# Windowed attention and a gated two-layer network on one core: output weights loaded in one piece ahead of the second batch, and a new table of order biases

## The chip, the cores and the metric

The kernel runs on one core of a Trainium2 chip, as one program. The metric is the device time in microseconds (us), the median of the runs shown. All data start and end in the chip's DRAM; loads, casts, transposes and stores are inside the time.

## The reference

For 8 batches, 8 heads, 576 positions and a head size of 64, the scores are `q @ k.T / 8`. Heads 0 to 3 ("plain") keep the 32 positions up to and including the row's own; heads 4 to 7 ("dilated") keep every fourth one of the last 128. A softmax over what is kept and a product with `v` give x, seen as 4608 tokens of 512 features (8 heads by 64).

Then comes the network, with `w_in` 512 x 2048, `beta` of 2048 and `w_out` 2048 x 512:

```python
h = x @ w_in
g = h * (1.0 / (1.0 + np.exp(-beta * h)))
return (g @ w_out).astype(np.float32)
```

All inputs and the output are float32; the kernel computes in bfloat16 with float32 sums.

## The kernel before, in words

**Two streams of work.** The network takes the tokens in 9 tiles of 512. For tile t, `slot_h` makes 16 blocks of 128 hidden features ("Ht", four matmuls of 128x512 each, L919); ScalarE takes a tanh (L928) and VectorE the gate (L933). `block` makes four output blocks ("Ot.0" to "Ot.3", 16 matmuls each in four parts, L954), evacuated at L969 or L971 and stored at L974. The attention of batch b must be done before the tiles that hold its 576 tokens: H1 needs batches 0 and 1, H2 batches 1 and 2, H3 batches 2 and 3, H4 batches 3 and 4, and so on.

**Attention of one batch.** Queries and keys must have their feature dimension on the partitions. For batches 0 to 2 (`b < DIRECT`) POOL's queue loads rows into `st` (`direct_qk`, L418), and TensorE turns them in four groups of 36 small matmuls (L502 dilated, L512 plain; 64 rows each), evacuated at L259. For batches 3 to 7 POOL's queue casts q and k into a DRAM scratch `s` (`cast`), and SP's queue brings them back by a transposing DMA (`crossbar`, L490). Then come scores (L715 dilated, L684 the last 64 positions of the dilated heads, L743 and L779 plain), exponentials on ScalarE (L651), masks (L655), products with the values (L805, L820, L836) and the normalization on VectorE (L670, L671). In batches 0 and 1 TensorE turns the result back into `xT` (L858, L873, L888, put at L259). From batch 2 on `back_dma` writes x to DRAM scratch (L539, L547, L552) and reads it back transposed, in two halves (L566), on SP's queue.

**What sets the order.** Nothing is reordered at run time: each engine and each DMA queue runs its instructions in program order and waits on semaphores. The program order is made at build time by the class `Plan`. Every operation states its engines with an assumed duration, its dependences and a due value `vt`. `Plan.run` keeps a clock for each engine and takes, among the operations that could start next, the one with the smallest `vt` within a small window of the earliest start. `NUDGE` adds a bias in nanoseconds to the start of single operations, named by their number in the order of creation. It only decides who goes first, and on engines that can both do an operation also which one does it. `late` adds to the landing that the plan assumes for some loads (values, rows, transposed loads) from the fifth batch on (`b > DIRECT`). `SWITCH` is the time that the plan charges TensorE when it passes between matmuls of 64 rows and others, as told by `halves`. Where the plan sees TensorE idle it puts in a filler matmul (L1067, 128x256, of zeros). So all these values change the order of instructions and the number of fillers, and nothing else.

**Loads.** POOL's queue holds, in order: batch 0's rows, batch 0's values, `w_in` (three pieces), then two pieces of `w_out` (`w_out_ld`, half of it each) among batch 1's loads. The place of the two pieces is set by their `vt` of -7.235 and -7.19; batch 1's loads have -7.25 to -7.19. The loads of batches 3 to 7 wait for one small copy on POOL (`t_pace`, L1033): batch 3's for the gate of the first H1 block, later ones for the previous batch's transposed loads and for the rows of `xT` two batches back.

Of the kernel before, what the change touches and what calls it, by code (L numbers as in the profile page):

```python
# [23 lines left out]


class Op:
    def __init__(self, engs, fn, deps, vt, acquire, group, dma, lat, halves=0, sbuf=False):
        self.halves, self.sbuf = halves, sbuf
        self.engs, self.fn, self.vt, self.acquire = engs, fn, vt, acquire
        self.deps = [d for d in deps if d is not None]  # L30
        self.dma, self.lat, self.group = dma, lat, group
        self.end = self.ready = None
        self.bias = 0.0
        self.late = 0
        self.waits = 0
        self.next = []
        for g in group if isinstance(group, list) else [] if group is None else [group]:
            g.users.append(self)


class Plan:
# [2 lines left out]


    CAPS = {"h": 4, "p": 4, "o": 3, "z": 4, "a": 8, "s": 5, "w": 6}
    SWITCH = 105
    NUDGE = {22: -150, 26: -150, 34: -150, 48: 400, 50: 400, 58: 400, 70: -150, 72: 2500, 84: 900,
        85: -2500, 86: -2500, 88: 2500, 89: 2500, 95: 60, 96: -60, 102: 60, 105: 150, 116: 2500,
        117: 150, 130: 400, 149: -400, 155: -60, 159: 900, 161: -60, 176: -150, 181: -400, 185: 60,  # L50
        187: -60, 191: 150, 196: 2500, 208: 60, 221: 2500, 227: -150, 228: -2500, 242: 150,
        251: 900, 252: 2500, 262: 400, 273: -2500, 291: -2500, 301: 400, 302: 150, 305: 900,
        316: -150, 323: 900, 358: 2500, 359: -60, 363: -60, 370: 150, 380: -60, 381: 2500,
        385: 150, 387: 2500, 388: -900, 417: -900, 422: -150, 423: -900, 429: -400, 442: 400,
        497: -60, 516: -2500, 524: 900, 526: 150, 536: 400, 540: 900, 541: -400, 542: 900,
        545: -900, 547: -2500, 556: -400, 559: -400, 579: -2500, 585: 900, 588: 900, 598: -400,
        659: -400, 660: 900, 664: 150, 665: 2500, 673: -400, 674: 2500, 675: 150, 680: -400,
        682: -400, 701: 60, 702: -900, 704: -150, 753: -400, 798: -400, 804: 150, 805: 900,
        806: 150, 807: 900, 808: 400, 818: 2500, 929: -60, 1058: 60, 1078: -150, 1084: 150,
        1105: 150, 1267: 2500}  # L60
    LAT = {"PE": 210, "ACT": 45, "DVE": 45, "POOL": 60, "SP": 0}
    NEAR = {"PE": 40, "ACT": 60, "DVE": 60, "POOL": 60, "SP": 0}

    def __init__(self, banks):
        self.ops, self.banks = [], banks

    def op(self, engs, fn, deps=(), vt=0.0, acquire=None, group=None, dma=0, lat=None, halves=0, sbuf=False, late=0):
        acquire = acquire if acquire is None or isinstance(acquire, list) else [acquire]
        o = Op(engs, fn, deps, vt, acquire, group or acquire, dma, lat, halves, sbuf)
        o.late = late  # L70
        o.bias = self.NUDGE.get(len(self.ops), 0)
        self.ops.append(o)
        return o

    def run(self, filler=None, filler_until=0.0):
# [11 lines left out]
        n_left = len(self.ops)  # L87
        n_held = {k: 0 for k in self.CAPS}
        ends = []
        halves = 0  # L90
        issued = 0.0
        port = {"DVE": 0.0, "POOL": 0.0}

# [19 lines left out]
        while n_left:  # L113
# [29 lines left out]
            if filler is not None and s <= filler_until and free["PE"] + (300 if free["PE"] < COLD else 170) < s:  # L143
                now = free["PE"]
                open_banks = {x.bank for x in held.values()}
                spare = [b for b, t in bank_free.items() if b not in open_banks and t <= now]
                if spare:
                    filler(max(spare, key=lambda b: -bank_free[b]))
                free["PE"] = now + (225 if now < COLD else 115)
                halves = 0  # L150
                continue
            for g in o.acquire or ():
                open_banks = {x.bank for x in held.values()}
# [5 lines left out]
            if e == "PE" and o.halves != halves:  # L159
                halves = o.halves  # L160
# [40 lines left out]
def kernel(  # L201
# [11 lines left out]
    P = 128  # L213
# [22 lines left out]
    DIRECT = 3  # L236
# [333 lines left out]
    def attention(b, ld, names, vts):  # L570
# [4 lines left out]
        if b < DIRECT:  # L575
            quarters = {}
            for n in [x for x in names if x[0] in "KQ"]:
                z, kind, i = "KQ".index(n[0]), n[1], int(n[2])
                vt = vt_of[n]
                srcs = ld["qk", z, 0 if kind == "P" else 4]  # L580
                srcs = srcs if isinstance(srcs, list) else [srcs]
                if i == 0:
                    gs = [Group("a") for _ in range(2)]
                    tr = plan.op([("PE", 36 * 8)],
                                 lambda e, gs=gs, z=z, t=t_quarters if kind == "P" else t_thirds: t(gs, z),
                                 srcs + [ident if kind == "P" else turn_op], vt, acquire=gs, halves=2)
                    quarters[kind, z] = gs, tr
                    used(("st", z), tr)
                g, tr = quarters[kind, z][0][i], quarters[kind, z][1]
                turned.append(tr)  # L590

                def evac(e, g=g, z=z, kind=kind, i=i):
                    tp = bank(g, BF16)[:, 0:S]
                    if kind == "P":
                        dst = qT[kv][:, i] if z else kT[kv][:, i, WIN:]
                        copy(e, dst.rearrange("p (g j) -> p g j", j=RP), tp.rearrange("p (j g) -> p g j", j=RP))
                    else:
                        copy(e, (dk, dq)[z][kv][:, :, 2 * i:2 * i + 2].rearrange("p r h (a o) -> p r (h a) o", o=RP),
                             tp.rearrange("p (r o u) -> p r u o", r=2, o=RP))
                key = (("kT", "qT")[z], kv, i) if kind == "P" else (("dk", "dq")[z], kv, i)  # L600
                steps[n] = [plan.op([dve(S), act(S)], evac, [tr, fill1] + war(key), vt, group=g)]
                wrote(key)
        else:
            ready = {"D": [ld["x", 0, 4], ld["x", 1, 4]], "P": [ld["x", 0, 0], ld["x", 1, 0], fill1]}
# [71 lines left out]
        for name in [n for n in names if n[0] in "ST"]:  # L676
# [24 lines left out]
            if x >= 2:  # L701
# [7 lines left out]
                def score(e, xs=xs, gs=gs):  # L709
                    for n, x in enumerate(xs):  # L710
                        for i in range(4):
                            r, h4 = i // 2, 2 * (x - 2) + i % 2
                            for c in range(2):
# [4 lines left out]
                deps = [o for n in ("KD0", "KD1", "QD0", "QD1") for o in steps[n]] if b < DIRECT else ready["D"]  # L718
                before = [plan.op([("PE", 2 * mm(4 * P))], added, [ident, adds["D"]], vt, acquire=gs)] if b < ADDED else []
                sop = plan.op([("PE", len(xs) * 4 * mm(P))], score, deps + before, vt,  # L720
                              acquire=None if before else gs, group=gs, halves=1)
                for r in range(2):
                    used(("dk", kv, r), sop)
                    used(("dq", kv, r), sop)
# [7 lines left out]
            if b >= AT_ONCE:  # L732
                if name != "S00":
                    continue
                gs = [Group("w") for _ in range(6)]

                def score(e, gs=gs):
                    for x in range(2):
                        for i in range(NI):
                            for h in range(2):  # L740
                                rows = slice(64 * h, 64 * h + 64)
                                n, at = divmod(at_once(x, i, h), 4)
                                nc.tensor.matmul(  # L743
                                    bank(gs[n])[:, at * QT:(at + 1) * QT], lhsT=kT[kv][rows, x, i * QT:i * QT + P],
                                    rhs=qT[kv][rows, x, i * QT:(i + 1) * QT], start=True, stop=True)
                sop = plan.op([("PE", 2 * NI * mm(QT))], score, [o for x in range(2) for o in steps[f"KP{x}"] + steps[f"QP{x}"]]
                              if b < DIRECT else ready["P"], vt, acquire=gs, halves=1)
                for x in range(2):
                    used(("kT", kv, x), sop)
                    used(("qT", kv, x), sop)  # L750
                old = [("pt", x, i) for x in range(2) for i in range(NI)] if b == AT_ONCE else []
                for n in range(6):
                    blocks = slice(4 * n, 4 * n + 4)
                    first = (1, 1, 5, 5, 2, 2)[n]
                    exp_and_mask(("P", n), sop, gs[n], vt, 4 * QT,
                                 lambda g=gs[n]: bank(g)[:, 0:4 * QT].rearrange("p (a n) -> p a n", n=QT),
                                 lambda blocks=blocks: pt_all[:, blocks, 0:QT],
                                 lambda first=first: mask_n[:, first:first + 4], [("pt", "P", n)] + old)
                continue
# [13 lines left out]
            def score(e, xs=xs, j=j, gs=gs):  # L773
                for n, x in enumerate(xs):
                    for a in range(3):
                        i = 3 * j + a
                        for h in range(2):
# [4 lines left out]
            before = [plan.op([("PE", 2 * mm(3 * QT) + 30)], added, [ident, adds["P"]], vt, acquire=gs)] if b < ADDED else []  # L782
            sop = plan.op([("PE", len(xs) * 3 * mm(QT))], score,
                          ([o for x in xs for o in steps[f"KP{x}"] + steps[f"QP{x}"]] if b < DIRECT else ready["P"]) + before,
                          vt, acquire=None if before else gs, group=gs, halves=1)
            for x in xs:
                used(("kT", kv, x), sop)
                used(("qT", kv, x), sop)
# [201 lines left out]
    for n in range(2):  # L990
        o = load("POOL", (w_out_bf[:, 8 * n:8 * n + 8, :],
                          moe_w_out[n * 8 * P:(n + 1) * 8 * P, :].rearrange("(c p) d -> p c d", p=P)),
                 [], (-7.235, -7.19)[n], 2048, .41)
        w_out_ld[2 * n] = w_out_ld[2 * n + 1] = o

    beta_ld = load("SP", (beta_row[:], moe_beta.rearrange("(f p) -> f p", p=P)), [], -9, 8)
# [104 lines left out]
```

## Time and profile before

| what | value |
|---|---|
| median of three runs (lowest, highest) | 303.25 us (302.43, 304.65) |
| the profiled execution's own time | 302.43 us |
| its span, first to last instruction | 300.7 us |
| TensorE (PE) busy | 290.8 us, 2460 matmuls, 39 of them fillers |
| VectorE (DVE), ScalarE (ACT), GpSimd (POOL) busy | 187.5, 169.8, 86.9 us |
| HBM read and written | 37.76 and 18.87 MB |
| granted TensorE clock | 1.00 |

The span is the profile's; 1.7 us of the execution's own time lie around it. Busy time of an engine says how long it ran, not that it ran usefully: fillers count. "Idle before" in a group is time that the engine stood still, with what ended it. A queue's line (SPq, POOLq) is the issue of a DMA; what it moves lands later, and the landing is the semaphore event that the trace holds. The packets of a transposing DMA are found in the trace by their size of 256 bytes, 1152 of them for each.

### The profile page before, as it was taken

To read this page: it belongs to the slowest core of one execution; us is meant where nothing else is said; L and a number is where in the kernel's file an instruction comes from. 1 tells how busy PE (TensorE), PEld (TensorE's weight loads), DVE (VectorE), ACT (ScalarE), POOL (GpSimd) and SP (SyncE) were. 2 spreads that over 40 slices of the span, in tenths; PEclk is the share of its full clock that TensorE was granted. 3 is DMA by queue.
4 is the path that set the end of the run, shared out by engine and by line. 5 is a ranking of instruction groups with operands and counts; after the bars stand their busy time and mean duration, and the time that the engine had idled before them with its cause. 6 is when DMAs were issued, how large, how long until landed. Compare 5 with 4: busy or idle time off the path is not lost.

```text
span 300.7 us, 6301 instructions
## 1 busy us (share of the span) xinstructions
PE 290.8 (97%) x2460; PEld 146.0 (49%) x2460; DVE 187.5 (62%) x425; ACT 169.8 (56%) x308; POOL 86.9 (29%) x127
## 2 busy tenths in 40 slices
PE   6799999999999988999999999999999999999996
PEld 4565456454454444454544454445454444444454
DVE  6678887778676746867668477566595056543300
ACT  4558866876546734675548374724673167554401
POOL 8958354783138008202730371000100000000000
PEclk9999999999999999999999999999999999999999
DMA  7999999999889999999899999555308200000122
GB/s 200 181 211 206 205 185 213 157 152 184 149 186 179 152 133 218 175 136 244 132 216 165 216 159 213 135 130 137 108 6 113 72 35 35 3 35 35 51 90 70
DMA packets 111009, 42.26 MB, mean 141 GB/s; under 512 B 87636, under 2 KB 103652, under 8 KB 110980
## 3 DMA queue, kind: packets, MB, share of 16 engines
q0 software_dynamic: 59488, 18.32, 59.3%
q1 hardware_dynamic: 51204, 23.18, 37.1%
q8 instruction: 19, 0.31, 0.4%
q10 hardware_dynamic: 288, 0.36, 0.3%
q14 instruction: 10, 0.08, 0.1%
HBM read 37.76 MB, written 18.87 MB: 188 GB/s over the span
## 4 chain that ended last, share of the span: by engine, by line
PE 86%; DMA 6%; SPq 4%; issue 1%; POOL 0%; ACT 0%; DVE 0%; POOLq 0%
PE bank L954 39%; PE bank L919 37%; DMA xT<-x 3%; SPq L490 2%; DMA st<-in_k_dram 2%; PE bank L836 2%; SPq L566 2%; PE bank L820 1%; DMA s<-in_k_dram 1%; PE bank L715 1%; PE bank L743 1%; PE bank L512 1%; PE bank L779 1%; PE bank L1067 1%; PE bank L805 1%
## 5 line engine op out<-in xcount | busy, mean ns | idle before, releaser
L954 PE MATMUL bank<-w_out_bf,g 128*128 128x512 bf16 (+2 forms) x608 | 136.9, 368 | 0.0
L919 PE MATMUL bank<-xT,w_in_bf 128*128 128x512 bf16 (+2 forms) x584 | 135.0, 376 | 1.9 <-DMA xT<-x 1.9
L933 DVE SCALAR_TENSOR_TENSOR g<-tnh,bank 128x512 bf16<-128x512 bf16 x144 | 96.2, 684 | 53.6 <-ACT tnh L928 52.6
L928 ACT ACTIVATE tnh<-bank,beta_half 128x512 bf16<-128x512 f32 x144 | 97.4, 689 | 55.5 <-PE bank L919 51.5
L919 PEld LDWEIGHTS <-w_in_bf 128*128 128x128 bf16 x584 | 55.3, 98 | 63.8 <-DMA xT<-x 2.0
L954 PEld LDWEIGHTS <-g 128*128 128x128 bf16 x608 | 55.2, 98 | 57.5
L969 ACT ACTIVATE osb<-bank 128x512 f32<-128x512 f32 (+1 forms) x31 | 18.2, 589 | 41.3 <-PE bank L954 37.3
L651 ACT ACTIVATE pt<-bank 128x384 bf16<-128x384 f32 (+1 forms) x54 | 20.3, 464 | 5.8 <-PE bank L779 3.6
L651 ACT ACTIVATE ptd<-bank 128x512 bf16<-128x512 f32 x32 | 16.9, 600 | 10.1 <-PE bank L715 10.0
L670 DVE RECIPROCAL rcp<-bank 128x4 f32<-128x4 f32 (+2 forms) x72 | 13.0, 180 | 12.6 <-PE bank L820 6.9
L655 DVE TENSOR_TENSOR ptd<-ptd,mask_d 128x512 bf16<-128x512 bf16 x27 | 11.4, 423 | 12.1 <-ACT ptd L651 11.2
L671 DVE TENSOR_TENSOR xsp<-bank,rcp 96x384 bf16<-96x384 f32 x32 | 17.7, 554 | 1.1
L655 DVE TENSOR_TENSOR pt<-pt,mask_n 128x384 bf16<-128x384 bf16 (+1 forms) x39 | 12.5, 346 | 6.2 <-ACT pt L651 5.7
L418 POOL DMA_DIRECT2D vt<-in_v_dram x16 | 14.1, 952 | 0.8 <-PE bank L684 0.8
L671 DVE TENSOR_TENSOR xdm<-bank,rcp 128x256 bf16<-128x256 f32 x32 | 13.6, 424 | 1.1
L655 POOL TENSOR_TENSOR pt<-pt,mask_n 128x288 bf16<-128x288 bf16 (+1 forms) x7 | 5.3, 771 | 30.4 <-ACT pt L651 30.4
L418 POOL DMA_DIRECT2D s<-in_q_dram x10 | 13.2, 1317 | 0.6 <-issue 0.6
L971 DVE TENSOR_SCALAR osb<-bank 128x512 f32<-128x512 f32 (+2 forms) x7 | 4.2, 593 | 14.1 <-PE bank L954 14.1
L259 POOL COPY qt<-dq 64x128 bf16<-64x128 bf16 x7 | 2.0, 290 | 34.9 <-DMA dq<-s 31.0
L418 POOL DMA_DIRECT2D s<-in_k_dram x10 | 11.7, 1169 | 0.3 <-issue 0.2
L418 POOL DMA_DIRECT2D vp<-in_v_dram x9 | 11.2, 1242 | 0.1
L836 PEld LDWEIGHTS <-pt 128*128 128x128 bf16 x192 | 8.5, 97 | 4.3
(117 smaller groups left out, 179.1 us busy)
## 6 DMA issues: line engine op xcount, KB each, us to landing
out_dram<-osb SPq DMA_DIRECT2D x35, 256.0 KB, 2.1
s<-in_k_dram POOLq DMA_DIRECT2D x10, 288.0 KB, 7.9
s<-in_q_dram POOLq DMA_DIRECT2D x10, 288.0 KB, 8.2
w_out_bf<-in_moe_w_out_dram POOLq DMA_DIRECT2D x2, 1024.0 KB, 17.4
vp<-in_v_dram POOLq DMA_DIRECT2D x7, 288.0 KB, 11.0
st<-in_q_dram POOLq DMA_DIRECT2D x6, 288.0 KB, 7.2
x<-xsp SPq DMA_DIRECT2D x12, 144.0 KB, 4.2
st<-in_k_dram POOLq DMA_DIRECT2D x5, 288.0 KB, 10.7
```

What stands on the lines that cost most here:

```text
L418: {"POOL": nc.gpsimd, "SP": nc.sync, "ACT": nc.scalar}[queue].dma_start(out=out, in_=in_)
L490: return plan.op([("SP", 1300)], lambda e: nc.sync.dma_start_transpose(out=dst, in_=src), deps, vt, dma=288 * 1024 / .2 / 1000, lat=5000, ...
L651: nc.scalar.activation(out=w(), in_=sc(), func=ACT.Exp, scale=SCALE)
L655: E[e].tensor_tensor(out=w(), in0=w(), in1=m(), op=ALU.mult)
L670: nc.vector.reciprocal(out=r, in_=p[..., D])
L671: nc.vector.tensor_tensor(out=dst, in0=p[..., 0:D], in1=r.unsqueeze(len(p.shape) - 1).to_broadcast(list(p.shape[:-1]) + [D]), op=ALU.mult)
L836: nc.tensor.matmul(pv[:, a, h2, :], lhsT=lhs, rhs=vp[kv][:, (2 * x + h2) * NI + 3 * j + a, 0:D + 1], start=True, stop=True)
L919: nc.tensor.matmul(bank(g)[:, a:z], lhsT=w_in_bf[:, kt, fb * P:(fb + 1) * P], rhs=xT[:, kt, xo + a:xo + z], start=(i == 0 and kt == kts[0] ...
L928: nc.scalar.activation(out=th[:, 0:n], in_=bank(g)[:, 0:n], func=ACT.Tanh, scale=beta_half[:, fb:fb + 1])
L933: nc.vector.scalar_tensor_tensor(out=g_t[t % 2][:, fb, c0:c0 + n], in0=th[:, 0:n], scalar=1.0, in1=bank(g)[:, 0:n], op0=ALU.add, op1=ALU.mult)
L954: nc.tensor.matmul(bank(g)[:, lo:hi], lhsT=g_t[t % 2][:, fb, tb * P:(tb + 1) * P], rhs=w_out_bf[:, fb, lo:hi], start=(fb == 0), stop=(fb = ...
L969: nc.scalar.mul(out=ob[:, lo:hi], in_=bank(g)[:, lo:hi], mul=0.5)
```

## The change

Four things differ.

1. The two pieces of `w_out` get the due values -7.27 and -7.26, so they follow `w_in` at once, ahead of all of batch 1's loads.
2. `NUDGE` is another table of biases (some 130 entries in each).
3. `SWITCH` is 95 instead of 105; `halves` is a truth value, and the transposes (L502, L512) no longer carry one: the plan sees a change of rows only at the scores.
4. The plan charges a group of 36 transposes with 306 ns instead of 288.

The `late` values, which the change's name speaks of, stand in both kernels. Every operation, its instructions and its sizes are the same; only order, choice of engine and fillers (45 instead of 39) differ.

```diff
-    SWITCH = 105
-    NUDGE = {22: -150, 26: -150, 34: -150, 48: 400, 50: 400, 58: 400, 70: -150, 72: 2500, 84: 900,
...
-        1105: 150, 1267: 2500}
+    SWITCH = 95
+    NUDGE = {11: 400, 34: -150, 35: 400, 36: -150, 43: -400, 61: -900, 62: 60, 63: -150, 70: 400,
...
+        952: -2500, 975: 900, 1063: -60, 1080: 2500, 1085: 150, 1185: -400}
...
-                    tr = plan.op([("PE", 36 * 8)],
+                    tr = plan.op([("PE", 18 * 17)],
                                  lambda e, gs=gs, z=z, t=t_quarters if kind == "P" else t_thirds: t(gs, z),
-                                 srcs + [ident if kind == "P" else turn_op], vt, acquire=gs, halves=2)
+                                 srcs + [ident if kind == "P" else turn_op], vt, acquire=gs)
...
     for n in range(2):
         o = load("POOL", (w_out_bf[:, 8 * n:8 * n + 8, :],
                           moe_w_out[n * 8 * P:(n + 1) * 8 * P, :].rearrange("(c p) d -> p c d", p=P)),
-                 [], (-7.235, -7.19)[n], 2048, .41)
+                 [], -7.27 + .01 * n, 2048, .41)
         w_out_ld[2 * n] = w_out_ld[2 * n + 1] = o
```

## The prediction

> **What bounds the kernel now.** I read first the page's busy shares, then busy time by stretch, then the chain that ended last, then POOL's timeline at the start.
>
> ```profile
> PE 290.8 (97%) x2460; PEld 146.0 (49%) x2460; DVE 187.5 (62%) x425; ACT 169.8 (56%) x308; POOL 86.9 (29%) x127
> DMA  7999999999889999999899999555308200000122
> ```
> TensorE (PE) is busy for all but 9.9 us of the 300.7. The DMA row matters as much: for 25 of the 40 slices (188 us) the DMA engines are nearly full, so a load that is asked for later also lands later.
>
> ```profile
> 0.00:22.00 22.00, 16.93 (x317) 11.48 (x318) 15.21 (x53) 11.90 (x26) 17.32 (x40) 1.00 1.17 197
> 22.00:60.00 38.00, 38.00 (x571) 20.02 (x570) 30.19 (x69) 29.20 (x60) 22.37 (x33) 1.00 1.31 193
> 60.00:90.00 30.00, 30.00 (x279) 15.37 (x278) 22.92 (x62) 18.12 (x37) 12.20 (x16) 1.00 1.35 168
> 90.00:120.00 30.00, 28.14 (x164) 13.13 (x163) 18.69 (x38) 16.85 (x27) 12.54 (x16) 1.00 1.49 169
> 120.00:150.00 30.00, 30.00 (x248) 14.98 (x247) 21.73 (x53) 18.87 (x36) 9.04 (x14) 1.00 1.39 172
> ```
> The second number is the stretch's length, the third PE's busy time. PE loses 5.07 us before 22, 1.86 between 90 and 120, nothing in between, and 2.9 at the very end. So only three places can give or take time: the start, the stall after 90, and new stalls where PE now has none.
>
> ```profile
> 100.75 4.96 SPq L566
> 105.81 7.92 DMA xT<-x
> 113.78 1.90 PE bank L919 x8
> ```
> These are pieces of the chain: start, length, what. The stall is H3 (first matmul 113.78), which waits for batch 3's second transposed load, issued at 105.81 on SP's queue and landed at 113.73.
>
> **The change, part by part.** Durations are those of this profiled execution; the order is that of the built changed kernel, which holds no times. To place an operation of the new order I add the step (start to next start) that each PE instruction ahead of it took in the trace.
>
> *Start.* Up to batch 0's last transposes (11.30) both orders wait for the same loads. Then VectorE's queue decides: its last normalization (L671) of batch 0 ends at 21.38, and the first matmul that needs it runs at 22.31, from where PE is full. The new VectorE queue has one put to `xT` and the evacuation of `beta` more there, and one mask less, +0.2 in the rows' durations. Followed link by link (value products, L670 and L671, transposes back, puts), the normalization ends near 21.8 and the matmul starts near 22.7: +0.4. Bounds -0.4 (the queue's waits, 0.9 and 0.7, half gone) and +1.2 (a ScalarE copy of 0.4 and a normalization of 0.75 more in line); I keep +0.4, nearest the queue's sum.
>
> *Fillers.* After that point the trace has 1 and the new order 4; consecutive ones step 0.11: +0.3.
>
> *Changes of rows.* An H or O part steps 0.86, and 0.96 ahead of 64-row matmuls. After the start the old order enters these 22 times, the new one 24 times, as the plan no longer sees the transposes: +0.2 (0 to +0.4, leaving included).
>
> *Batch 1 in VectorE's queue.* The new order moves `vd`'s spread (0.43) from POOL to VectorE, ahead of two masks (0.37 each) and of batch 1's first normalizations. From the evacuation of the last transposes (42.6) they add to 47.7, and PE wants to turn the result back (L873) at 47.1: +0.6 (0 to +1.0).
>
> *`w_out` ahead of batch 1.* The landings step by 5.05 and 5.09 for the pieces of `w_out`, 1.46 for dilated keys, 0.3 for each of two `vt`, 1.36 and 1.4 to 1.5 for the other three.
>
> ```profile
> 10.99 1.50 POOL L418 DMA_DIRECT2D w_in_bf<-in_moe_w_in_dram  x2
> 12.48 0.56 POOL L418 DMA_DIRECT2D st<-in_k_dram  x1
> 13.01 0.70 POOL L418 DMA_DIRECT2D vt<-in_v_dram  x1
> 13.69 0.57 POOL L418 DMA_DIRECT2D st<-in_q_dram  x1
> 14.22 0.92 POOL L418 DMA_DIRECT2D w_out_bf<-in_moe_w_out_dram  x1
> ```
> (Start, length of the issue; the landings come 12 to 19 us after it, since the queue is full.) `w_in`'s end moves from 24.48 to about 24.2, as one `vt` leaves the front; then `w_out` ends at 34.3 and the first keys of batch 1 at 35.8, where they were at 25.94. PE needed them at 28.42. The new order puts all of H0 and two parts of O0 ahead: 13.7 us of steps after 22.7, so 36.4. Margin 0.6; for the next three groups 37.8 against 38.7, 39.3 against 40.3, 40.7 against 42.0. Batch 2's first group lands at 48.3 and is wanted at 49.4. So this costs nothing by the rows; its cover is H0, and if a landing slips by more than 0.6 PE pays all of the rest. By 44.5 the same bytes have landed in both orders.
>
> *The stall at 113.8.* The new order puts the whole of O2 ahead of H3, whose first matmul comes at 120.5. Batch 3's transposed loads are now last of six on SP's queue; in the trace the six ended at 115.8, and they start 0.5 later (below): about 117. So the wait goes: -1.9. Late next is H3's operand by -3.6, that is, nothing.
>
> *Elsewhere.* From H8 to the end the two orders are alike. Between, H4 (wanted 150.4, loads at about 145) and batch 5's plain scores (148.9 against 142) have room.
>
> Sum: +0.4 +0.3 +0.2 +0.6 -1.9 = -0.4. Of some ten hand-overs from SP's queue to PE the trace lost 1.9 us at one; the new order has four with 2 to 4 us of margin (batch 3's scores, H2, batch 4's scores, H3), for which I add 0.4. That makes no change: own time 302.4, and as the median lies 0.8 above the profiled execution, **303.2 us**. What a measurement of this kernel can tell from no change is about 1%, 3 us.
>
> **The rivals.**
>
> *Batch 3's rows come late (slower).* The loads of batch 3 wait for the gate of H1's first block:
>
> ```profile
> 54.91 0.31 POOL L1033 COPY pace<-g 1x2 bf16<-1x2 bf16 x1 [2.07 <-DVE g L933]
> 55.17 0.61 POOL L418 DMA_DIRECT2D s<-in_k_dram  x1
> ```
> H1 starts at 52.38 in the trace and at 57.3 in the new order (batch 1's work and O0 stand ahead), so this goes from 54.91 to 59.8 and all of batch 3's loads by 4.9 us. The last cast, at 72.63, lands at 77.5. Behind it SP's queue now holds the plain queries' transposed load and both of batch 2's `xT` halves; H2 wants the second at 90.7. In the trace these three ran when POOL's loads were over and their packets took 3.3, 1.9 and 2.3 us; so they end near 88.5, margin 2.2, and that speaks against. Against POOL's loads (97 to 110) the same sizes took 5.1, 4.3 and 3.4. At that pace they end at 92.5 and land at 93.0; H2 waits 2.3, and batch 4's loads, which are paced by that landing, go by 4.5 and bring up to 1 more at H3. Price +3, time 306.2; it decides from the point where the second half lands after 90.7.
>
> The Trainium skill, "DMA: Bandwidth & Descriptors", section "Latency and other measured facts", gives 261 GB/s for transposing DMAs; for 288 KB that is an estimate of 1.1 us each, and the rival would have no price at all. The trace agrees only for loads that ran alone (1.1 to 1.6 us late in the span) and not next to POOL's, so I go by the rows.
>
> *Batch 1's rows come late.* If `w_out` takes longer than 5.05 and 5.09 in a row, the first transposes wait, as nothing but SP's idle queue runs beside. 1 us more makes 304.2 after the margin of 0.6 and the later waits that it swallows; for it speaks the thin margin, against it that `w_in`'s last piece of the same size took 4.96.
>
> *The stall goes and nothing comes (faster).* Start -0.4, no wait in batch 1, no hand-over lost: -0.4 +0.3 +0.2 -1.9 = -1.8, so 301.4. For 1% the start's own 5.07 us would have to shrink by 1.3 beyond that, and they wait for loads that do not move.
>
> *The change doesn't do what its name says.* The late landings stand in both kernels; priced at nothing, it leaves the parts above.
>
> **How the numbers follow.** Forecast (waits traded for one another, 302.0 to 304.3): 0.58. Batch 3 late (304.8 to 307): 0.24. Batch 1 late (304 to 305.5): 0.09. Faster rival (300 to 302): 0.09. The range takes in the price of the first rival and most of the faster one: 301.5 to 306.6. Below 300.2 lies 0.05. Above 306.3 lie half of the first rival (0.12), both late rivals together (0.03) and waits of the two elementwise queues that I have not followed (0.05): 0.2. The rest, 0.75, is within 1%.
>
> **What would show it.** Right: no PE idle between 90 and 120; H3 near 120; the first copy at L1033 near 60; L502 of batch 1 at about 36 with no wait on `st`; PE's idle time in the first 22 us near 5. Wrong: PE waiting for `xT<-x` near 91, with L566 packets above 3 us each; PE waiting for `st` near 36 or 49; a first H0 matmul later than 20; or short waits on L651 and L671 in batches 1 to 3 that add to more than 1 us, as ScalarE's and VectorE's queues are ordered anew throughout and I have followed only where the sums came out tight. A stall longer than some 3 us would cost more than itself by a rule of the Trainium skill, "TensorE: Matmul & The Clock Gate", section "What's actually happening": after an idle window of about 3.4 us the array runs at half speed. The trace's stall of 1.9 left the granted clock at 1.00, and no run here shows a longer one.

## The result, and the profile after

The changed kernel takes **302.12 us** (median; 301.74 to 303.21). The kernel before, measured beside it, takes 304.92 us (302.18 to 306.69). The ratio is 0.992, with a 95% interval of 0.9899 to 0.9941: a gain of 0.8%, inside the 1% that the prediction called no change, and 1.1 us under the predicted 303.2. The interval leaves 1 out, so there is something to explain. The two profiled executions give no hint of it: 302.55 us after, 302.43 before. What differs is the spread, 1.5 us after and 4.5 us before.

The page of the changed kernel (busy time and share of each engine; DMA load in 40 slices). Its line numbers are 3 higher than those of the kernel before: L505 is L502 there, L922 is L919, L957 is L954.

```profile
PE 293.4 (98%) x2466; PEld 148.0 (49%) x2466; DVE 183.7 (61%) x420; ACT 170.2 (57%) x309; POOL 91.5 (30%) x131
DMA  7999999489999999999899999999206200100122
```

TensorE is busy for 2.6 us more in a span that is 0.1 us longer, so its idle time has fallen from 9.9 to 7.4 us; 2.9 us of both lie at the very end. The DMA row stays full longer, to the end of slice 28 (25 before), since batch 3 and all behind it are asked for later.

Busy time by stretch (stretch, length, PE, PEld, DVE, ACT, POOL with counts, granted clock, DMA share, GB/s), after:

```profile
0.00:22.00 22.00, 17.75 (x317) 11.74 (x318) 14.86 (x53) 11.52 (x25) 18.06 (x41) 1.00 1.15 198
22.00:60.00 38.00, 37.80 (x570) 21.02 (x569) 27.82 (x66) 28.00 (x56) 18.47 (x26) 1.00 1.23 180
60.00:90.00 30.00, 30.00 (x259) 14.99 (x257) 20.41 (x53) 17.85 (x36) 15.13 (x19) 1.00 1.27 167
90.00:120.00 30.00, 30.00 (x211) 14.43 (x210) 20.61 (x46) 16.89 (x31) 13.08 (x17) 1.00 1.40 177
```

The stretch from 90 to 120, where TensorE lost 1.86 us, is full. The same view had 28.14 there. TensorE's waits, after (what waited, for what: sum, times, longest):

```profile
PE bank L1070 <- DVE warm L321: 1.1, 1, 1.1
PE bank L505 <- DMA st<-in_q_dram: 1.1, 1, 1.1
PE bank L823 <- issue: 0.6, 1, 0.6
```

Ahead of the end these and four smaller ones are all there is, and all but one of 0.17 us lie in the first 22 us. TensorE's timeline, after, at the two places the sum turned on (start, busy, line, shapes):

```profile
34.80 1.03 PE L957 MATMUL bank<-w_out_bf,g 128*128 128x512 bf16 x4
35.76 0.48 PE L505 MATMUL bank<-turn,st 64*64 64x64 bf16 x36
...
120.29 1.04 PE L957 MATMUL bank<-w_out_bf,g 128*128 128x512 bf16 x4
121.16 1.03 PE L922 MATMUL bank<-xT,w_in_bf 128*128 128x512 bf16 x4
```

Batch 1's first keys are turned at 35.76 with no wait (they landed at 35.35), and H3 begins at 121.16 right behind O2 (the packets of its last load end at 117.73).

### The profile page after: what moved, and what is told of

The parts are those of the page before. It is cut to its first block, busy times and chain, and to the rows that moved or that the text cites. A ratio compares the mean times of both kernels' runs of the same rounds, so it can differ in the third digit from the quotient of the medians.

```text
span 300.8 us, 6299 instructions
## 1 busy us (share of the span) xinstructions
PE 293.4 (98%) x2466; PEld 148.0 (49%) x2466; DVE 183.7 (61%) x420; ACT 170.2 (57%) x309; POOL 91.5 (30%) x131
## 4 chain that ended last, share of the span: by engine, by line
PE 93%; DMA 2%; DVE 2%; ACT 1%; issue 1%; POOL 0%; POOLq 0%; DVEq 0%
PE bank L957 42%; PE bank L922 40%; DMA st<-in_k_dram 2%; PE bank L839 2%; PE bank L718 2%; PE bank L823 1%; PE bank L746 1%; PE bank L515 1%; PE bank L1070 1%; PE bank L808 1%; DVE g L936 1%; PE bank L782 1%; PE bank L505 1%; PE bank L687 1%; PE bank L891 0%
## 5 line engine op out<-in xcount | busy, mean ns | idle before, releaser
L957 PE MATMUL bank<-w_out_bf,g 128*128 128x512 bf16 (+2 forms) x608 | 137.4, 368 | 0.0
L922 PE MATMUL bank<-xT,w_in_bf 128*128 128x512 bf16 (+2 forms) x584 | 134.7, 376 | 0.1
L922 PEld LDWEIGHTS <-w_in_bf 128*128 128x128 bf16 x584 | 55.5, 98 | 61.9 <-issue 0.3
L957 PEld LDWEIGHTS <-g 128*128 128x128 bf16 x608 | 55.1, 98 | 57.4 <-issue 0.3
L972 ACT ACTIVATE osb<-bank 128x512 f32<-128x512 f32 (+1 forms) x33 | 19.4, 593 | 37.4 <-PE bank L957 37.1
L654 ACT ACTIVATE pt<-bank 128x384 bf16<-128x384 f32 (+1 forms) x54 | 21.7, 468 | 11.3 <-PE bank L746 8.1
L658 DVE TENSOR_TENSOR pt<-pt,mask_n 128x384 bf16<-128x384 bf16 (+1 forms) x35 | 13.3, 384 | 15.6 <-ACT pt L654 15.2
L1036 POOL COPY pace<-xT 1x2 bf16<-1x2 bf16 x4 | 0.9, 214 | 42.1 <-DMA xT<-x 42.1
L974 DVE TENSOR_SCALAR osb<-bank 128x512 f32<-128x512 f32 (+2 forms) x5 | 2.8, 557 | 16.9 <-PE bank L957 16.9
L421 POOL DMA_DIRECT2D s<-in_k_dram x10 | 12.8, 1278 | 0.7 <-issue 0.6
L421 POOL DMA_DIRECT2D s<-in_q_dram x10 | 12.2, 1224 | 0.3 <-issue 0.3
L658 POOL TENSOR_TENSOR pt<-pt,mask_n 128x288 bf16<-128x288 bf16 (+1 forms) x11 | 10.9, 1056 | 4.5 <-ACT pt L654 4.5
```

The lines of the kernel that those rows point to most:

```text
L421: {"POOL": nc.gpsimd, "SP": nc.sync, "ACT": nc.scalar}[queue].dma_start(out=out, in_=in_)
L654: nc.scalar.activation(out=w(), in_=sc(), func=ACT.Exp, scale=SCALE)
L658: E[e].tensor_tensor(out=w(), in0=w(), in1=m(), op=ALU.mult)
L922: nc.tensor.matmul(bank(g)[:, a:z], lhsT=w_in_bf[:, kt, fb * P:(fb + 1) * P], rhs=xT[:, kt, xo + a:xo + z], start=(i == 0 and kt == kts[0] ...
L957: nc.tensor.matmul(bank(g)[:, lo:hi], lhsT=g_t[t % 2][:, fb, tb * P:(tb + 1) * P], rhs=w_out_bf[:, fb, lo:hi], start=(fb == 0), stop=(fb = ...
L972: nc.scalar.mul(out=ob[:, lo:hi], in_=bank(g)[:, lo:hi], mul=0.5)
```

## The experiments

The gain cannot be read from the two profiles, so the experiments ask where the spread of the kernel before comes from, and what the parts of the change do alone. In all of them the order of either kernel is written out as a list, so that only the steps named in the diff move, with the steps of ScalarE and VectorE that belong to them. The list raises the line numbers by 55 to 59: L974 (or L975, L978) is L919 of the front, L557 is L502, L770 is L715, L875 is L820, L1009 (or L1013) is L954. Steps have the names of the front: "O2.2 p0" is the first quarter of output block O2.2 (four 128x512 matmuls), H3.5 a hidden block of H3, F a filler. "Before" in these runs means the kernel before on the same chip.

### The kernel before twice more

No edit; the program is the one before. The question is what its trace looks like when the time is longer.

> The kernel before, its order written out as a list, instruction for instruction the same; a second profiled execution. Theory A (batch 3's late landing ahead of H3 varies from execution to execution): own time near 305, idle time of PE before 22 us as in the first profile (5 us, within 0.5), and the wait of H3 on L566 grown from 1.9 to about 4 us. Rival B (the start varies): the wait at H3 stays near 1.9 and the first 22 us hold some 2 us more idle. Rival C (several hand-overs): new waits at batch 1's or 2's transposes, H2 or the scores of batches 3 to 5 that add to 2 us or more.

> The same kernel once more, for a third profiled execution: theory A, B and C as for the second one; under A the differences of own time between the three profiles follow the differences of the wait at H3 one for one.

Measured: 304.0 us (span 302.3) and 304.49 us (span 302.8), both with a mean granted clock of 0.994, which is what one stretch of 3.41 us at half clock leaves over 302 us. Waits of TensorE in the first:

```profile
PE bank L974 <- DMA xT<-x: 2.0, 1, 2.0
PE bank L1122 <- DVE warm L373: 1.1, 1, 1.1
PE bank L974 <- issue: 1.1, 1, 1.1
PE bank L557 <- DMA st<-in_q_dram: 0.9, 1, 0.9
```

H3's wait is 1.96 us, hardly more than the 1.86 of the first profile, in an execution 1.6 us longer; the 4 us of theory A are not there. The stretches around it show what else was lost:

```profile
107.46:110.87 3.41, 3.41 (x17) 1.37 (x15) 0.95 (x2) 0.00 (x0) 0.00 (x0) 1.00 1.83 158
110.87:114.29 3.42, 1.41 (x23) 0.93 (x24) 1.47 (x4) 2.40 (x5) 0.22 (x2) 1.00 1.26 139
114.29:117.70 3.41, 3.41 (x13) 1.41 (x12) 0.61 (x2) 0.69 (x1) 3.41 (x5) 0.50 1.00 188
```

I cut the stretches where the trace's clock record changes. TensorE is busy for 1.41 us of the middle one, and for the whole of the next it is granted half the clock: a 128x512 matmul takes 635 ns there instead of 380, and H3's first seven take 3.03 us, where the first profile's eight took 1.90. Laid beside the first profile matmul by matmul, TensorE is 1.3 us ahead by 22 us; it loses 1.1 in a gap at 54.4 us (the third wait above, inside a block of H1, for which the trace names no cause), 0.1 in H3's wait and 1.7 in the stretch of half clock. In the second run H3 waits 2.51 us, and there is a new wait:

```profile
PE bank L974 <- DMA xT<-x: 2.5, 1, 2.5
PE bank L557 <- DMA st<-in_q_dram: 1.6, 1, 1.6
PE bank L770 <- DVE g L988: 1.6, 1, 1.6
```

Its stretch of half clock is at the start:

```profile
4.84:8.26 3.42, 1.55 (x42) 0.63 (x40) 1.56 (x4) 1.45 (x3) 3.28 (x7) 1.00 1.14 222
8.26:11.67 3.41, 3.32 (x88) 2.10 (x90) 1.93 (x5) 1.54 (x3) 3.14 (x8) 0.50 1.83 174
```

It follows a wait of 1.62 us for `st<-in_q_dram`. But this stretch did not make the run longer: by 22 us TensorE is 0.1 us ahead of the first profile. The 2.1 us come from the wait of 1.58 us at 77.6, ahead of batch 3's first scores (L770), and from 0.65 more at H3. Ahead of those scores ScalarE got batch 3's transposed queries only at 75.94 us (73.81 in the first profile), and its tanh and VectorE's gates, the last that TensorE waited for, came behind. That wait is a lost hand-over, as in rival C; theory A has only the 0.65.

What follows: a wait of some 2 us can cost a stretch of half clock on top, in one execution and not in another. In the first repeat, among full matmuls, that stretch cost 1.7 us; in the second, at the start, nothing that lasted. Over the 79 runs of the kernel before beside the experiments, 30 had a mean clock of 0.999 or 1.0 and a median of 303.13 us, and 49 had 0.983 to 0.994 and a median of 304.74. All 30 runs of the changed kernel (20 for the result, 10 below) had 0.998 or more. Where the stretch lies in the 49 is not known, and that it is what made them longer is not shown: of the two repeats, which are of this kind, it made one longer.

### H3 behind eight parts of O2, and behind three

The part of the change that the prediction priced highest, alone: some of O2 ahead of H3, the rest of the order as before.

```diff
  scores of batch 4 (dilated)
+ O2.2 p0 p1 p2 p3, O2.3 p0 p1 p2 p3      (second kernel: O2.2 p0, O2.3 p0, O2.2 p1)
  H3.5, H3.0, H3.1 ... with the value products between
- these parts of O2 between the blocks of H3
```

> The order of before, in which the eight parts of O2.2 and O2.3 take the PE places ahead of the blocks of H3 and these the later ones; attention keeps its places. H3 starts near 118.8 instead of 113.8. Theory A: no wait at H3, median 300.5 to 302, and the runs lie within 1.5 us of each other. Rival B or C: only the 1.9 us of the first profile goes, median 302.5 to 303.5, and the runs still spread over 3 us or more.

> The order of before, with three parts of O2 (O2.2 p0, O2.3 p0, O2.2 p1, four 128x512 matmuls each, 0.86 us by the timeline, 2.6 us in all) ahead of H3's first block in place of behind it. If the wait at H3 costs its own 1.9 to 2.5 us and the clock's window besides, both go: no wait at H3, clock at least 0.999 outside the start, profiled time 300.4 to 301.2 and median 300.7 to 301.6, under the changed kernel. If what the wait gives back is taken again by the steps behind it (gate and hidden values late, as with eight parts moved), 302.4 to 303.1 as there.

Measured: with eight parts 302.98 us (302.53 to 304.16), ratio 0.9961 (0.9933 to 0.9989); with three 302.12 (301.88 to 303.28), ratio 0.995 (0.9926 to 0.9973). No wait at H3 in either, and all twenty clocks at 0.999 or 1.0. Both miss the gain that the wait alone promised; with three the time lies between the two bands of its expectation. With eight parts H3's blocks stand so close that TensorE waits for gates and exponentials at 125 to 135 us instead (0.41, 0.29 and 0.57 us). With three, one wait of TensorE stands behind H3's first blocks:

```profile
PE bank L875 <- DVE ptd L710: 1.3, 1, 1.3
```

It is the value product of batch 4's fourth dilated tile. That tile's exponential and mask stand behind H3's first tanh and gate in the queues of ScalarE and VectorE, and H3 now comes later. Both profiles also have the gap inside H1 at about 55 us (1.10 and 0.95 us). In the four profiles of before's order that have 0.5 us or more of it (the first repeat, these two, and 16 fillers below), TensorE is 0.5 to 1.3 us ahead of the first profile until then and within 0.2 of it behind: what the start had gained is lost again.

What follows: moving 2.6 us of O2 ahead of H3 gives the whole time of the changed kernel (302.12 in both; 302.31 for the changed kernel beside these runs). None of the other parts of the change is needed for it. The two give back what they gain in different places, so that they agree to the last digit is chance.

### The same, with the waiting tile ahead of H3's first gate

```diff
  three parts of O2 ahead of H3, as above
+ ScalarE: exponential of batch 4's fourth dilated tile, VectorE: its mask
  ScalarE: tanh of H3.0, VectorE: gate of H3.0
- the same two steps here
```

> The order of before with the three O2 parts ahead of H3, and in addition the fourth dilated score tile of batch 4 exponentiated on ScalarE and masked on VectorE ahead of H3's first tanh and gate, in place of behind them (ScalarE waits there 3.5 us for H3's first block anyway). It takes away the 1.29 us for which TensorE waited for that tile (bank<-vd,ptd at 120.08). If that wait is what ate the gain, the profile has no TensorE wait over 0.5 us between 23 and 297 us, its span is 299.0 to 299.5 and the median 300.7 to 301.3, under the changed kernel's 302.1 to 302.3. If the wait only stood in for another (the hidden blocks' tanh and gates are what TensorE waits for in the end), 301.8 to 302.3.

Measured: 301.84 us (300.91 to 302.52), ratio 0.9904 (0.9873 to 0.9936). Four of nine runs had a clock of 0.999 or more and lie at 300.91 to 301.70; the other five, at 0.989 to 0.994, at 301.84 to 302.52. The profile is of the second kind. Its largest waits:

```profile
PE bank L557 <- DMA st<-in_q_dram: 1.4, 1, 1.4
PE bank L1122 <- DVE warm L373: 1.1, 1, 1.1
```

The 1.3 us wait is gone, and nothing over 0.5 us is left behind the start. The forecast of 300.7 to 301.3 holds for two of the four runs at full clock (300.91 and 301.20). The median missed it by 0.5 us through stretches of half clock at the start:

```profile
5.04:8.45 3.41, 1.74 (x77) 0.87 (x75) 1.26 (x3) 1.68 (x3) 3.27 (x7) 1.00 1.10 201
8.45:11.86 3.41, 3.41 (x84) 1.99 (x71) 2.03 (x5) 2.10 (x4) 3.21 (x8) 0.50 1.75 174
```

There they are cheap, 0.7 us between the medians of the two kinds, probably since TensorE waits for loads between short steps anyway; no run tests that. The intervals of this kernel and of the changed one overlap, so it is not shown to beat it; its four runs at full clock all lie below the changed kernel's lowest (301.70 and less against 301.74).

### Fillers in front of the wait

The order of before, with fillers where TensorE waits for H3's operand. Nothing arrives sooner.

```diff
  scores of batch 4 (dilated)
+ F x 16                                   (second kernel: F x 28)
  H3.5, H3.0 ...
```

> The order of before, with 16 of its filler matmuls (128x256 on zeros, some 0.115 us each, 1.8 us in all) ahead of H3's first block; nothing else moves, and the load that H3 waits for lands when it did. If the time lies in the waiting alone, the work is the same and the wait is only painted over: median 304 to 305 and a spread of some 3 us, as before. If it is the clock that falls after the wait, TensorE stays busy over the stretch from 113 to 116 us: mean granted clock at least 0.999 in nearly all runs (a window of half clock is left only at the start), median 302.7 to 303.3 and a spread under 2 us, though work was added and no data come earlier.

> The order of before with 28 fillers (some 3.3 us) in place of 16 ahead of H3, so that TensorE has work until after the load of batch 3's rows has landed in every run. If a wait of about 1 us in front of H3 is what still set the clock back with 16 fillers, all ten clocks are now at least 0.999 and the runs lie within 1.6 us of each other, at 303.0 to 304.0 (the fillers end later than the load in some runs). If the half clock comes from the start, whose order is the same, or if fillers of zeros don't count as work, clocks of 0.988 to 0.994 stay in half of the runs, as with 16.

Measured: 303.41 us (302.41 to 304.22, ratio 0.9979, 0.9952 to 1.0006) with 16; 303.64 (303.04 to 305.39, ratio 0.9984, 0.9952 to 1.0017) with 28. The clock was 0.999 or more in four of ten runs with 16 fillers, and in seven of ten with 28. The profile with 16 still has a wait of 0.97 us at H3, behind 1.9 us of fillers, and no stretch of half clock. The profile with 28 has no wait there, and its stretch of half clock is at the start:

```profile
4.92:8.33 3.41, 1.53 (x46) 0.60 (x44) 1.49 (x3) 1.51 (x3) 3.31 (x6) 1.00 1.13 213
8.33:11.74 3.41, 3.41 (x90) 2.19 (x92) 1.97 (x5) 1.66 (x4) 3.14 (x8) 0.50 1.75 171
```

What follows: with 16 fillers the spread (1.8 us) is what the clock's expectation said, the median is 0.1 above its band, and its forecast for the clocks failed: six runs stayed under 0.999. In those six the time is hardly longer (medians 303.53 and 303.34), as it is where the stretch lies at the start, but they were not profiled, so the place is not shown. With 28 the clocks came between the two expectations. Work that gives nothing made the kernel no slower, but both intervals just take in 1, so a gain is not shown. What is left open is the start: its order is the same in all kernels made from the order of before, and yet no run of twenty fell under 0.999 with eight or three parts of O2 moved, five of nine with the early tile, and six of ten with 16 fillers.

### The changed kernel again, and without its fillers at the start

```diff
  F x 18
  ...
- F x 27, singly or in groups of up to 6, between later steps
```

> The changed kernel again, on the same chip as the three others. If its time is steady because no wait of TensorE behind the start is longer than 0.2 us: median 301.9 to 302.4, all runs within 1.6 us, mean granted clock at least 0.999 in every run. If its steadiness was chance, some of its runs lie at 303.5 or more with a clock of 0.994 or less.

> The order of after, without the 27 fillers behind the first 18 (some 3.7 us of filler work in the first 22 us). If those fillers only fill waits, nothing changes but the waits: first full matmul at 22.0 to 22.6, median 301.6 to 302.2, clock 1.00. If they keep the clock up, the waits of 1 to 2.5 us at the start bring a window of half clock (3.4 us) in many of the runs: mean clock 0.988 to 0.995 there, median 303 to 304.5, spread over 2 us.

Measured: again 302.31 us (301.94 to 303.61), all ten clocks 0.998 or more. Without the fillers 302.71 (301.67 to 304.42): three runs at 0.999 with 301.67, 301.73 and 302.88 us, and seven at 0.977 to 0.994 with a median of 302.81. The median stays under the 303 to 304.5 that was expected with a falling clock. Its profile is of the first kind (span 300.0).

What follows: the fillers hold the clock, in 30 of 30 runs against three of ten. What that is worth is less sure: the medians differ by 0.4 to 0.6 us, but the intervals overlap (0.9921 to 0.9968 with them, 0.9926 to 0.9992 without), and where the clock holds without them two of three runs lie at 301.7, so they may cost some 0.4. One part of after_again's expectation failed: its runs lie within 1.7 us, and one at 303.61 with a clock of 1.0, so not all of the spread is clock.

### The place of `w_out`, alone

Two kernels separate the place of the two `w_out` loads on POOL's queue from the order on TensorE that goes with it.

```diff
 first kernel, order of before:            second kernel, order of after:
  w_in                                      w_in
+ w_out, w_out                            - w_out, w_out
  batch 1's loads                           batch 1's loads
- w_out, w_out among them                 + w_out, w_out among them
```

> The order of before with one thing changed: both pieces of w_out follow w_in on POOL's queue, as in the changed kernel. Batch 1's first keys land near 35.5 instead of 25.9, and PE wants them at 28.4 with nothing to put in: it waits 7 us, later groups wait little more, time 309 to 312. If the place of the pieces is harmless by itself, 303 to 305.

> The order of after, with the two loads of w_out put back on POOL's queue to where before has them (behind batch 1's loads). The first hidden-to-output blocks, which after starts with, then wait: the second half lands near 41.9 us as in before, while O0's third part is wanted at 37.2. Wait of about 4.8 us there and, if a wait of that length sets the clock back as the 8.3 us one did, a stretch of half clock behind it: 307 to 309, clock 0.985 to 0.995. If the load's place doesn't matter, 302 to 303 and no wait.

Measured: 313.0 us (312.55 and 313.46; ratio 1.027) for the first and 309.11 (308.98 and 309.24; ratio 1.0158, 1.0086 to 1.023) for the second, 1.0 and 0.1 us above the expected bands. TensorE's longest wait in the first, and then its stretches from the beginning of that wait on:

```profile
PE bank L557 <- DMA st<-in_k_dram: 8.3, 1, 8.3
```

```profile
27.53:30.94 3.41, 0.34 (x2) 0.00 (x0) 0.66 (x2) 0.69 (x1) 3.21 (x7) 1.00 1.24 208
30.94:34.36 3.42, 0.00 (x0) 0.00 (x0) 0.00 (x0) 0.00 (x0) 0.94 (x1) 0.50 1.28 207
34.36:37.77 3.41, 1.42 (x45) 1.29 (x47) 0.80 (x2) 0.87 (x2) 1.35 (x2) 0.50 1.19 204
37.77:41.18 3.41, 3.41 (x41) 1.22 (x41) 1.41 (x4) 1.39 (x3) 0.00 (x0) 0.50 1.69 184
41.18:44.60 3.42, 3.37 (x51) 1.64 (x41) 2.98 (x6) 2.58 (x6) 1.89 (x5) 1.00 1.05 69
```

Three stretches at half clock, only the last of which is full of work. In the second kernel O0 waits for its weights:

```profile
PE bank L1013 <- DMA w_out_bf<-in_moe_w_out_dram: 3.8, 1, 3.8
```

```profile
38.46:41.88 3.42, 0.58 (x3) 0.29 (x3) 0.00 (x0) 0.00 (x0) 0.00 (x0) 1.00 1.86 179
41.88:45.29 3.41, 3.41 (x51) 1.56 (x48) 0.94 (x2) 0.93 (x2) 0.00 (x0) 0.50 2.15 171
```

A wait of 3.8 us, a stretch of half clock, and 6.8 us more than the changed kernel (309.11 against 302.31).

What follows: the two parts are worth nothing apart. The early `w_out` needs H0 and O0 ahead of batch 1 on TensorE, and that order needs the early `w_out`. Together they hide all of it, as forecast.

### Fillers at the start of the best order

```diff
  the order with three parts of O2 and the early tile
+ F x 10 ahead of the second turn of batch 0's keys
+ F x 6 ahead of the second step of batch 0's pooled scores
```

> The one before the last (three O2 parts ahead of H3, batch 4's tile masked early) with 16 fillers more at the start: 10 ahead of the second turn of batch 0's keys, where TensorE waits 1.44 us for st<-in_q at 8.2 us, and 6 ahead of the second step of batch 0's pooled scores. There its profile has a window of half clock from 8.45 to 11.86 us, and five of its nine runs have a clock of 0.989 to 0.994 and lie 0.7 us higher than the four at 0.999 (300.9 to 301.7). If the wait at the start is what sets the clock back, the fillers (1.1 us and 0.7 us, both inside waits) take the windows away: all clocks at least 0.999, median 301.0 to 301.6, spread under 1.3 us. If the fillers hold up the steps behind them by as much as they save, or the window comes from the wait that is left (0.3 to 0.5 us), 301.7 to 302.2.

Measured: 302.96 us (302.36 to 305.08), ratio 0.996 (0.9935 to 0.9985). Twelve of thirteen clocks are 0.999 or more, but these twelve have a median of 302.93, where the kernel without the fillers had 301.43 at that clock. The one profile is of the remaining run, the slowest; the wait for `st` is gone from it, and a new one stands behind, ahead of a mask product for batch 0 (L765 of the front):

```profile
PE bank L821 <- issue: 1.8, 1, 1.8
```

```profile
12.70:16.11 3.41, 1.65 (x23) 1.08 (x21) 1.94 (x7) 0.58 (x2) 3.25 (x5) 1.00 1.25 204
16.11:19.52 3.41, 3.41 (x32) 2.39 (x32) 0.79 (x3) 1.73 (x5) 1.25 (x5) 0.50 1.17 213
```

What follows: the stretches of half clock went, and the fillers cost 1.5 us for the 0.7 that such a stretch costs there, which is worse than the rival expected (301.7 to 302.2). The two kernels ran on different chips, beside medians of before of 304.53 and 304.44. What L821 waits for the trace does not name, nor a second gap of 1.59 us at 56.6, inside a group of 36 small transposes; and it shows only the one run with half clock, so where the 1.5 us went is open.

## Why the prediction was right, and where it was not

**The class and the range.** A change under 1% was given 0.75, and 302.12 lies in the range and in the forecast's own band (302.0 to 304.3). The own time of the profiled execution was forecast at 302.4 and is 302.55.

**The stall at 113.8 gone, -1.9.** Right. H3 was placed at 120.5 with its loads at about 117; the trace has 121.16 and 117.73. Three parts of O2 alone reproduce the whole time of the changed kernel. This is the step that carries the result.

**`w_out` ahead of batch 1, nothing.** Right, and as thin as it was said to be. Keys landed at 35.35 (35.8 forecast) and were wanted at 35.76 (36.4): margin 0.4 for 0.6. With the cover gone the price was 8.3 or 3.8 us of wait and half clock besides.

**Start, +0.4.** First full matmul at 22.59 against 22.31, +0.28 for +0.4; waits of the first 22 us 4.25 instead of 5.07.

**Fillers +0.3 and changes of rows +0.2.** The term that was mis-sized. From the first full matmul to the end the changed trace is 0.17 us shorter. With the stall's 1.86 gone and 0.17 of new wait, its steps took 1.5 us more where I had 0.5. Step by step against the old trace, nearly all of it lies between 39 and 57 us, where batch 1's attention is cut into smaller groups and mixed anew:

```profile
44.74 0.29 PE L823 MATMUL bank<-vd,ptd 128*128 128x65 bf16 x4
44.95 0.30 PE L782 MATMUL bank<-qT,kT 64*128 64x96 bf16 x6
...
62.25 0.28 PE L823 MATMUL bank<-vd,ptd 128*128 128x65 bf16 x4
62.38 0.59 PE L922 MATMUL bank<-xT,w_in_bf 128*128 128x512 bf16 x2
```

A group of four value products takes 0.22 us to the next start when 64-row matmuls follow (44.74) and 0.12 between full matmuls (62.25): the same 0.10 that an H or O part loses there. I counted 22 and 24 of these entries, as those of H and O parts; behind any matmul the traces have 23 and 26, nine of the 26 behind small groups. That is 0.3 us, and the fillers took 0.2. The rest goes with the finer cut: 64-row groups of six take 0.22, where groups of twelve took 0.36, and some 0.4 besides the wait itself went at the 0.17 us wait at 45.66.

**Batch 1 in VectorE's queue, +0.6.** Not seen: TensorE's only wait there is 0.17 us, at 45.66. The hand-overs' 0.4 was not seen either, though the second repeat of before shows that one can be lost (1.58 us). These two cancelled the mis-sized term, so the sum was right by compensation, which is luck.

**Batch 3's rows late (rival, 0.24).** Did not come. The first copy at L1036 ran at 60.47 (59.8 forecast), so the casts did move. But the loads behind them are quick: their packets took 1.08, 1.46 and 1.50 us, where I took 3.3, 1.9 and 2.3. The second half of H2's operand ended at 87.39 (88.5 forecast), and H2 began at 91.19: margin 3.8 for 2.2. The figure of the Trainium skill's "DMA: Bandwidth & Descriptors" in "Latency and other measured facts", an estimate of 1.1 us for each, was nearer here than the slow rows that I preferred. The two halves ahead of H3 took 1.66 and 1.06. My reading of the old trace, 1.1 to 1.6 us late in the span, had left out slower ones there, up to 3.2.

**Batch 1's rows late, and the faster rival.** The first had its decisive point at a slip of 0.6, and none came. The second (301.4) needed a start 0.4 us earlier and no new cost in the middle. The start's waits did shrink, by 0.8, but more work stands there and the first full matmul came 0.28 later; and the middle cost 1.5. Neither happened.

**From the profile to the median, +0.8.** This is the step that failed, and why 303.2 was 1.1 too high. I carried the distance between before's profiled execution and its median over to the changed kernel, as if it were a property of the measurement. It belongs to the kernel: more runs put before's median 2.1 to 2.5 us above that execution, and after's is 0.4 below its own. With three parts of O2 ahead of H3, and nothing else, the median falls by 2.4 us (304.54 to 302.12) and the clock holds in all ten runs, so the stall is worth more than the 1.9 that I read from one profile. What the slower runs of before lost besides is in part open. Beside the experiments the median of before is 304.53; its 30 runs at full clock have 303.13; the changed kernel, in 30 runs, has 302.17. So 1.4 us of the difference goes with the clock and 1.0 with the rest. But that split rests on sorting runs by their clock, and it is not the clock's price: one repeat lost 1.7 us to half clock behind the stall, the other none, but 1.5 at a late hand-over at 77.6 us and 0.65 in a longer stall.

**The rule about idle TensorE.** I wrote that an idle stretch of some 3 us would be needed and that 1.9 left the clock at 1.00. The second was true of one execution only. The same wait in the same program, 1.96 us long, brought half clock in another.

## What to carry to other kernels

A wait of TensorE is not priced by its length alone: at 2 us it can bring 3.41 us of half clock behind it (1.7 us of time here), in some executions and not in others. So before a distance between profile and median is called noise, read the granted clock of every run and profile more than one: the two repeats here lost their time in different places. Put ready work ahead of the late operand, just enough of it, and look next at what was queued behind the moved step on the other engines. Moving a load and moving its consumer are one edit: each alone cost 7 to 8 us here.

## What the runs showed of the hardware

The clock records change only at whole multiples of 3.413 us from the record's start, which lies 3.9 to 7.1 us after the span's start and differs from run to run; ahead of the last matmul, half clock lasted one such stretch (3.41 us) in six profiles and three (10.24 us) in one; seven have none. The Trainium skill's "TensorE: Matmul & The Clock Gate", section "What's actually happening", describes such a free-running window of 3413 ns, and the runs agree with it. They differ on the idle time that is needed: the page names a whole idle window, and here no stretch had to be idle. Half clock followed when TensorE was busy for 0.00 to 1.74 us of a stretch, about half of it or less. It did not follow at 1.81 us (at H3, with the early `w_out` alone) or 1.84 (second repeat, at 76.5), nor at 2.22, as in the first profile of before, where the same wait fell on two stretches:

```profile
109.69:113.10 3.41, 2.22 (x27) 1.10 (x25) 1.36 (x3) 1.93 (x4) 0.00 (x0) 1.00 1.86 119
113.10:116.51 3.41, 2.73 (x17) 1.31 (x18) 1.41 (x5) 1.16 (x3) 2.33 (x4) 1.00 1.21 241
```

One stretch speaks against a sharp bound, in the second repeat of before, where H3 waited 2.51 us:

```profile
114.07:117.48 3.41, 1.58 (x7) 0.80 (x9) 1.19 (x4) 0.92 (x3) 1.23 (x3) 1.00 1.05 153
117.48:120.89 3.41, 3.41 (x35) 1.88 (x33) 2.17 (x7) 2.45 (x4) 3.41 (x5) 1.00 1.07 172
```

It was busy for 1.58 us and the next kept the full clock. So a half-empty stretch is what to avoid; exactly how much work saves it is not settled by these runs.
